# Walking the slices of d_ff two by two in a fused attention and MLP kernel

## The chip, the cores and the metric

The kernel runs on one core of one Trainium2 chip. The metric is the device time of one execution in microseconds. Five engines work side by side, each through its own instructions in order: PE (TensorE, matmuls; PEld is its loading of the stationary operand), DVE (VectorE), ACT (ScalarE), POOL (GpSimd) and SP (SyncE, which here issues nearly all DMAs).

## The reference

```python
# q, k, v: (4, 8, 768, 64); banded attention with 8 global and 96 local keys, slopes by head
scores = scale * q @ k.T + bias                    # bias = -slope * distance
a = softmax(where(keep, scores, -1e9))             # keep: the band and the global keys
attn_out = a @ v
x = attn_out.transpose(0, 2, 1, 3).reshape(3072, 512)
h = x @ w_in                                       # w_in: (512, 2048)
g = h * clip(h + 3, 0, 6) / 6
out = g @ w_out                                    # w_out: (2048, 512)
```

## The kernel before, in words

The 3072 tokens are eight blocks of 384. For a block, four pairs of heads are attended, each giving 128 rows of the transposed x; then the MLP runs over 16 slices of d_ff, 128 columns each. A matmul operand is split in a high and a low part, both in fp32r, and three of the four products are summed. Per slice that makes:

- the first layer (`first`, L167): four k-tiles by three products, 12 matmuls of 128x128 by 128x384 into one PSUM tile `hp`. There are two `hp` banks.
- the gate: ACT takes relu(h+3) into `g` (L178), DVE makes min(g, 6)\*h (L179), POOL copies the high part `gh` (L185) and DVE takes the rest `gl` = g - gh (L192). There is one `g` tile (pool `gp1`); `gh` and `gl` have three buffers each (pool `gp`).
- the second layer (`second`, L199): three tiles of 128 tokens by three products, 9 matmuls with 512 output columns, into the three `acc` tiles (for the second block, the tiles `sp`, `tp` and `xp`).

`halves` walks the slices with a lag of one: first layer of slice f, a yield, then the second layer of slice f-1 (`finish`), a yield. After the last slice of a block `finish` also stores the block: three ACT copies to tiles `o` (pool `op`, three buffers), three DMAs. The lag goes over the edge of a block: the last slice of a block gets its second layer inside the first slice of the next.

At each yield the caller hangs in a unit of the attention for the block after: `attention` spreads four pairs over 30 units, six a pair. Units 0, 1 and 2 of a pair are the score matmuls of the token tiles t = 0, 1, 2 (L842, four matmuls each) with their weighing (DVE L853, ACT L857); unit 3 splits the next pair's q and k (`kx` on POOL L813), sums up and normalizes two tiles (POOL L877), unit 4 normalizes the third and spreads the first, unit 5 spreads the others and fetches. `spread` turns the softmax rows by DVE in blocks of 32 (L902) and writes them to DRAM by a DMA (L904, `there<-blocks`); `fetch` reads them back, transposed, by four DMAs (L911, `weights<-there`). At the ends of the second and the fourth pair (units 17 and 29) `values` multiplies those weights by v for two pairs (L929, here called values) and writes x. During the last eight slices of the second block `rest_of_third` does the same for the third block in coarser units.

A scheduler orders DVE and ACT; PE, SP and POOL keep the order in which the program is written (`in_order`). The weights are decoded from int64 words during the first 155 us, on DVE above all; in that time the slices of the first two blocks go in an order written by hand (`ORDER`), and that part stays as it is.

Of the kernel before, what the change touches and what calls it, by code (L numbers as in the profile page):

```python
# [25 lines left out]
NF = DF // P  # L26
# [33 lines left out]
class Kernel:  # L60
# [45 lines left out]
    def common(self, xs, banks):  # L106
        self.xp = self.pool("xp", xs)
        self.w1h, self.w1l, self.w2h, self.w2l = [], [], [], []
        self.gp = self.pool("gp", 3)
        self.gp1 = self.pool("gp1", 1)  # L110
        self.ps_h = self.pool("ps_h", banks, PSUM)

# [174 lines left out]
    def load(self, n, values):  # L287

        if n < len(self.blocks) * NPAIR:
            end = KW + (TB if n < EARLY else QW)  # L290
            for columns in (slice(KW + QW, LOAD),) if values else (slice(0, KW), slice(KW, end)) if n == 0 else (slice(0, end),):
                self.nc.sync.dma_start(out=self.place(n)[:, columns], in_=self.pairs[n, :, columns])
# [155 lines left out]
    def halves(self, steps, pool=False):  # L448


        for block, f, x, acc in steps:
# [11 lines left out]
                yield  # L463
            self.last = (block, f, acc, gh, gl)

    def end(self, steps):

        x, acc = steps[0][2:]
        late = []
        for k, (_, f, _, _) in enumerate(steps):  # L470
            g = self.gate(self.first(f, x), f == NF - 1)
            gh = self.high(g, True)
            late.append((f, acc, gh, self.rest(g, gh)))
            if k == 0:
                self.finish()
            elif k == 1:
                self.second(*late[0], (0, 1))
        self.second(*late[0], (2,))
        self.second(*late[1], (0, 1))
        self.second(*late[2], (0, 1))  # L480
        self.second(*late[1], (2,))
        self.second(*late[2], (2,))
# [11 lines left out]
    def banded(self, flag):  # L494
# [12 lines left out]
        with ExitStack() as early, ExitStack() as words:  # L507
            x0 = self.x_tiles(self.pool("x0", 1, ctx=early, side="right"))
            xs = [x0, self.x_tiles(), self.x_tiles()]
# [7 lines left out]
            acc = []  # L517
# [62 lines left out]
            acc1 = [pool.tile([P, BANK], F32, name=name) for pool, name in ((self.ps_s, "sp"), (self.ps_t, "tp"), (self.ps_x, "xp"))]  # L580
            self.given[1] = max(self.given)
            next_f, todo = [FIRST, 0], []
# [6 lines left out]
        self.attending(self.ctx, 2, 3, 2, side="right")  # L589
        self.bp = self.pool("bp", 3, side="right")  # L590
        self.there = self.pool("there", 2, bass.MemoryType.DRAM)
        self.op = self.pool("op", 3, side="right")
        self.stage = "one"
        units, pairs = self.rest_of_third(xs[2], NF - next_f[1])
        for k, _ in enumerate(self.halves([(1, f, xs[1], acc1) for f in range(next_f[1], NF)], True)):
            for unit in units[k]:
                unit()
        self.finish()
        pairs[-2].values("s")
        self.stage = "layers"  # L600
        x, ahead = xs[2], pairs[-1]
        for i in range(2, len(self.blocks)):
            units, x_next = [], None
            if i + 1 < len(self.blocks):
                x_next = self.x_tiles()
                units, ahead = self.attention(i + 1, x_next, ahead)
            else:
                units = [[]] * 4 + [[lambda: self.doubt(flag)]]
            acc = self.acc_tiles()
            steps = [(i, f, x, acc) for f in range(NF)]  # L610
            for k, _ in enumerate(self.halves(steps if x_next else steps[:-3], True)):
                for unit in units[k] if k < len(units) else ():
                    unit()
            if not x_next:
                self.end(steps[-3:])
            x = x_next
# [392 lines left out]
```

## Time and profile before

| | |
|---|---|
| median of 3 runs | 663.02 us (662.13 to 663.42) |
| span of the profiled execution | 660.9 us, from its first to its last instruction |
| PE | 649.6 us busy, 98% of the span |
| PEld | 581.9 us, 88% |
| DVE | 427.6 us, 65% |
| ACT | 288.1 us, 44% |
| POOL | 202.2 us, 31% |

The profile is of one execution. Its time by the clock that gave the three runs isn't listed, so durations are set against the span of 660.9 us; the median is 2.1 us above it. Busy times overlap: matmuls are pipelined, a row's duration is longer than the distance from its start to the next one's, so the pace of PE is read from starts. The word "pitch" stands for that distance below.

### The profile page before, as it was taken

The numbers are of one execution on the slowest core, as the hardware profiler recorded it, in microseconds if no ns is written. First come the engines' busy times: TensorE is split into PE (matmuls) and PEld (weight loads), VectorE is DVE, ScalarE is ACT, GpSimd is POOL, SyncE is SP. The second block draws the span as 40 slices with busy tenths as digits, with TensorE's granted clock in tenths as the row PEclk, the third lists the DMA queues.
The fourth block names the chain that finished last, engine by engine and source line by source line (L and its number), as shares of the span: only waits on it lengthen the run. The fifth ranks groups of instructions, "written<-read, shape, count | busy, mean of one in ns | idle before, by whom it ended". The sixth has DMA issues, their size and how long they took to land.

```text
span 660.9 us, 11414 instructions
## 1 busy us (share of the span) xinstructions
PE 649.6 (98%) x3933; PEld 581.9 (88%) x3933; DVE 427.6 (65%) x1147; ACT 288.1 (44%) x752; POOL 202.2 (31%) x377
## 2 busy tenths in 40 slices
PE   9989999999999999999999999999999999999997
PEld 7768899998989999999989999899998999989995
DVE  6888999998856876367654777367663777422222
ACT  6896877776434343344314333143422443121111
POOL 5663000002533433034331553134340444312110
PEclk9999999999999999999999999999999999999999
DMA  8676445432582566536553557615654265510001
GB/s 284 178 233 215 132 157 159 132 124 89 158 224 95 156 175 172 143 100 162 153 153 96 135 137 185 180 51 143 165 138 128 95 160 131 133 49 1 1 1 53
DMA packets 67316, 88.86 MB, mean 134 GB/s; under 512 B 10288, under 2 KB 52016, under 8 KB 67248
## 3 DMA queue, kind: packets, MB, share of 16 engines
q1 hardware_dynamic: 66960, 87.77, 46.5%
q8 instruction: 33, 0.54, 0.3%
q14 instruction: 35, 0.29, 0.1%
q10 hardware_dynamic: 288, 0.26, 0.1%
HBM read 65.08 MB, written 22.94 MB: 133 GB/s over the span
## 4 chain that ended last, share of the span: by engine, by line
PE 86%; DVE 9%; ACT 2%; issue 2%; POOL 0%; POOLq 0%; DVEq 0%; ACTq 0%
PE hp L167 37%; PE acc L199 33%; PE xp L929 3%; PE sp L842 2%; PE tp L929 2%; PE tp L842 2%; PE sp L199 1%; ACT n L857 1%; DVE wz L422 1%; PE tp L199 1%; DVE wz L418 1%; PE xp L199 1%; DVE wz L410 1%; DVE g L179 1%; DVE gl L192 1%
## 5 line engine op out<-in xcount | busy, mean ns | idle before, releaser
L178 ACT ACTIVATE g<-hp,small 128x384 f32<-128x384 f32 x127 | 73.7, 580 | 253.3 <-PE hp L167 227.0
L167 PE MATMUL hp<-xh,w1h 128*128 128x384 f32 x512 | 174.1, 340 | 0.4 <-ACT w1h L426 0.4
L167 PE MATMUL hp<-xh,w1l 128*128 128x384 f32 x512 | 173.0, 338 | 0.5 <-DVE w1l L415 0.5
L167 PE MATMUL hp<-xl,w1h 128*128 128x384 f32 x512 | 171.9, 336 | 0.0
L185 POOL TENSOR_SCALAR gh<-g 128x384 fp32r<-128x384 f32 x104 | 55.6, 535 | 311.2 <-DVE g L179 279.7
L199 PE MATMUL acc<-w2h,gl 128*128 128x512 f32 x336 | 133.2, 396 | 0.2 <-DVE gl L192 0.2
L199 PE MATMUL acc<-w2l,gh 128*128 128x512 f32 x336 | 132.4, 394 | 0.0
L199 PE MATMUL acc<-w2h,gh 128*128 128x512 f32 x336 | 131.9, 393 | 0.0
L179 DVE SCALAR_TENSOR_TENSOR g<-g,hp 128x384 f32<-128x384 f32 x128 | 69.8, 545 | 69.7 <-ACT g L178 69.1
L877 POOL TENSOR_SCALAR n<-n,sums 128x232 f32<-128x232 f32 (+1 forms) x186 | 99.4, 549 | 32.2 <-DVE sums L868 17.6
L192 DVE TENSOR_TENSOR gl<-g,gh 128x384 fp32r<-128x384 f32 x128 | 78.4, 613 | 47.5 <-POOL gh L185 47.5
L857 ACT ACTIVATE n<-n,least 128x232 f32<-128x232 f32 (+1 forms) x192 | 89.0, 465 | 41.6 <-DVE least L853 40.3
L167 PEld LDWEIGHTS hp<-xh,w1h 128*128 128x128 f32 x512 | 96.3, 188 | 6.4 <-issue 1.7
L167 PEld LDWEIGHTS hp<-xl,w1h 128*128 128x128 f32 x512 | 96.2, 188 | 3.8
L167 PEld LDWEIGHTS hp<-xh,w1l 128*128 128x128 f32 x512 | 96.0, 188 | 1.0 <-DVE w1l L415 0.8
L199 PEld LDWEIGHTS acc<-w2h,gl 128*128 128x128 f32 x336 | 63.0, 187 | 15.1 <-DVE gl L192 1.6
L199 PEld LDWEIGHTS acc<-w2h,gh 128*128 128x128 f32 x336 | 63.3, 188 | 10.5 <-POOL gh L185 0.3
L199 PEld LDWEIGHTS acc<-w2l,gh 128*128 128x128 f32 x336 | 63.2, 188 | 10.3
L902 DVE STREAM_TRANSPOSE blocks<-n 128x256 f32<-128x256 f32 x127 | 48.8, 422 | 27.0 <-POOL n L877 26.8
L813 POOL TENSOR_SCALAR kx<-load 64x504 fp32r<-64x504 f32 (+1 forms) x46 | 35.3, 767 | 100.3 <-PE hp L167 96.2
L853 DVE CUSTOM_DVE_ANT_0 n<-sp,d 128x232 f32<-128x232 f32 (+1 forms) x70 | 23.7, 376 | 36.7 <-PE sp L842 36.5
L857 ACT ACTIVATION_READ_ACCUMULATOR n<-n,least 128x1 f32 x192 | 36.1, 188 | 0.0
(118 smaller groups left out, 746.4 us busy)
## 6 DMA issues: line engine op xcount, KB each, us to landing
wst<-w SPq DMA_DIRECT2D x32, 512.0 KB, 3.5
there<-blocks SPq DMA_DIRECT2D x58, 256.0 KB, 2.6
load<-pairs SPq DMA_DIRECT2D x23, 636.0 KB, 5.1
load<-pairs SPq DMA_DIRECT2D x32, 384.0 KB, 4.3
weights<-there SPq DMA_DIRECT2D x48, 192.0 KB, 3.8
weights<-there SPq DMA_DIRECT2D x44, 160.0 KB, 3.2
out<-o SPq DMA_DIRECT2D x23, 256.0 KB, 2.2
load<-pairs SPq DMA_DIRECT2D x8, 444.0 KB, 4.4
```

Of the source, the lines that this page charges most:

```text
L167: self.nc.tensor.matmul(hp, lhsT=self.w1(w, f)[:, kt, :], rhs=a[:, kt, :], start=(n == 0), stop=(n == 3 * NKT - 1))
L178: nc.scalar.activation(out=g, in_=hp, func=AF.Relu, bias=self.three, scale=1.0)
L179: nc.vector.scalar_tensor_tensor(out=g, in0=g, scalar=6.0, in1=hp, op0=ALU.min, op1=ALU.mult)
L185: self.nc.gpsimd.tensor_scalar(out=gh, in0=g, scalar1=1.0, scalar2=0.0, op0=ALU.mult, op1=ALU.add)
L192: self.nc.vector.tensor_tensor(out=gl, in0=g, in1=gh.bitcast(F32), op=ALU.subtract)
L199: self.nc.tensor.matmul(acc[tt], lhsT=a[:, tk], rhs=self.w2(w, f), start=(f == 0 and j == 0), stop=(f == NF - 1 and j == 2))
L813: nc.gpsimd.tensor_scalar(out=part["kx"][own, c], in0=k[own, c], scalar1=1.0, scalar2=0.0, op0=ALU.mult, op1=ALU.add)
L842: nc.tensor.matmul(sp[j][:, lo:W], lhsT=q[:, t], rhs=part["kx"][:, c], start=(m == 0), stop=(m == 1))
L857: nc.scalar.activation(out=e[:, j, lo:W], in_=e[:, j, lo:W], func=AF.Exp, bias=self.least[:, i:i + 1], scale=-1.0, accum_out=self.sums[:, ...
L877: nc.gpsimd.tensor_scalar(out=e[:, j, lo:W], in0=e[:, j, lo:W], scalar1=over, scalar2=0.0, op0=ALU.mult, op1=ALU.add)
L902: nc.vector.transpose(out=blocks[:, :, s].rearrange("p b j q -> p j b q"), in_=e[:, :, c:c + P].rearrange("p j (b q) -> p j b q", b=4))
L929: nc.tensor.matmul(xps[j * D:(j + 1) * D, t * P:(t + 1) * P], lhsT=vt[0:K, t, j * D:(j + 1) * D], rhs=self.part(t, j, c, K), start=(c == 0 ...
```

## The change

A new walker `twos` takes the slices in pairs: both first layers with their gates, two yields, then the second layers of the pair before, two yields. It takes the place of `halves` from slice 8 of the second block to the end, but for the last three slices of the last block, which `end` still walks one by one. `gh` and `gl` get a fourth buffer each, and `o` goes from three buffers to two to make room. No instruction is added or taken away: each engine issues the same number of each operation up to the end of this path.

```diff
-        self.gp = self.pool("gp", 3)
+        self.gp = self.pool("gp", 4)
...
+    def twos(self, steps, pool=False):
+        for i in range(0, len(steps), 2):
+            after = []
+            for block, f, x, acc in steps[i:i + 2]:
+                self.decoded_to(2 * f)
+                g = self.gate(self.first(f, x))
+                gh = self.high(g, pool)
+                after.append((block, f, acc, gh, self.rest(g, gh)))
+                self.work(2.1, 0.94)
+                if i == 0 and len(self.pending) == 1:
+                    self.last = self.pending[0]
+                    self.finish()
+                    self.pending = []
+            yield
+            yield
+            for self.last in self.pending:
+                self.finish()
+            self.pending = after
+            yield
+            yield
...
     def end(self, steps):
...
             if k == 0:
-                self.finish()
+                for self.last in self.pending:
+                    self.finish()
...
-        self.op = self.pool("op", 3, side="right")
+        self.op = self.pool("op", 2, side="right")
...
-        for k, _ in enumerate(self.halves([(1, f, xs[1], acc1) for f in range(next_f[1], NF)], True)):
+        self.pending = [self.last]
+        for k, _ in enumerate(self.twos([(1, f, xs[1], acc1) for f in range(next_f[1], NF)], True)):
...
-        self.finish()
+        for self.last in self.pending:
+            self.finish()
+        self.pending = []
...
-            for k, _ in enumerate(self.halves(steps if x_next else steps[:-3], True)):
+            for k, _ in enumerate(self.twos(steps if x_next else steps[:-3], True)):
```

On PE, in a late block, before: the end of a slice's first layer (tile `hp_5570`) and the second layer of the slice before it.

```order
L167 MATMUL hp_5570<-xh_4119,w1h1_1023 128x384
L167 MATMUL hp_5570<-xl_4120,w1h1_1023 128x384
L167 MATMUL hp_5570<-xh_4119,w1l1_1024 128x384
L199 MATMUL acc_4951<-w2h1_1025,gh_5531 128x512
L199 MATMUL acc_4951<-w2l1_1026,gh_5531 128x512
L199 MATMUL acc_4951<-w2h1_1025,gl_5543 128x512
```

On PE after, in the same block: the end of a first layer is followed by the next slice's.

```order
L167 MATMUL hp_5506<-xh_4110,w1h1_1023 128x384
L167 MATMUL hp_5506<-xl_4111,w1h1_1023 128x384
L167 MATMUL hp_5506<-xh_4110,w1l1_1024 128x384
L167 MATMUL hp_5526<-xh_4110,w1h1_1023 128x384
L167 MATMUL hp_5526<-xl_4111,w1h1_1023 128x384
L167 MATMUL hp_5526<-xh_4110,w1l1_1024 128x384
```

The runs of one kind are now 24 and 18 matmuls long instead of 12 and 9. From slice 8 of the second block on there were 104 runs of first layers and 104 of second layers; now there are 55 and 54. The score matmuls, which stood between them four at a time, stand eight and four at a time: `yield` follows on `yield`, so units 0 and 1 of a pair come together.

On POOL, around the normalizing of the last pair of heads of a block, before (`kx` of the next pair, `n` the softmax rows, `gh` the gates):

```order
L185 TENSOR_SCALAR gh<-g 128x384 x2
L813 TENSOR_SCALAR kx<-load_73 64x504 x2
L877 TENSOR_SCALAR n<-n,sums 128x128 x2
L877 TENSOR_SCALAR n<-n,sums 128x232 x2
L185 TENSOR_SCALAR gh<-g 128x384
L877 TENSOR_SCALAR n<-n,sums 128x232 x2
```

On POOL after, at the same place:

```order
L185 TENSOR_SCALAR gh<-g 128x384 x2
L839 TENSOR_SCALAR kx<-load_73 64x504 x2
L903 TENSOR_SCALAR n<-n,sums 128x128 x2
L903 TENSOR_SCALAR n<-n,sums 128x232 x4
L185 TENSOR_SCALAR gh<-g 128x384 x6
```

The six normalizings now follow on each other; before, a gate's copy stood ahead of the last two.

On DVE, at the same pair, before: from the split of the next pair's q (the two rows on L816) to the turning of the softmax rows (`blocks`).

```order
L816 SCALAR_TENSOR_TENSOR q_5555<-load_73,q_5554 128x384
L816 SCALAR_TENSOR_TENSOR q_5560<-load_73,q_5559 128x384
L192 TENSOR_TENSOR gl<-g,gh 128x384
L867 TENSOR_SCALAR sums<-sums 128x6
L819 TENSOR_TENSOR kx<-load_73,kx 64x504
L868 RECIPROCAL sums<-sums 128x6
L819 TENSOR_TENSOR kx<-load_73,kx 64x504
L902 STREAM_TRANSPOSE blocks<-n 128x2x4x32
L179 SCALAR_TENSOR_TENSOR g<-g,hp 128x384
L902 STREAM_TRANSPOSE blocks<-n 128x2x4x32 x2
L192 TENSOR_TENSOR gl<-g,gh 128x384
L902 STREAM_TRANSPOSE blocks<-n 128x2x4x32 x2
```

On DVE after:

```order
L842 SCALAR_TENSOR_TENSOR q_5556<-load_73,q_5555 128x384
L842 SCALAR_TENSOR_TENSOR q_5561<-load_73,q_5560 128x384
L179 SCALAR_TENSOR_TENSOR g<-g,hp 128x384
L893 TENSOR_SCALAR sums<-sums 128x6
L894 RECIPROCAL sums<-sums 128x6
L192 TENSOR_TENSOR gl<-g,gh 128x384
L845 TENSOR_TENSOR kx<-load_73,kx 64x504 x2
L928 STREAM_TRANSPOSE blocks<-n 128x2x4x32 x5
```

The gate of the second slice of the pair now stands ahead of the sums, the reciprocal no longer behind a split of `kx`, and no gate between the turnings.

## The prediction, made before the changed kernel ran

> **What bounds the kernel now.** I read the busy times first, then the same by stretches of the part that changes, then the pitch of PE's matmuls in the timeline, and last the chain that feeds the values. The page says that PE is busy for 98% of the span:
>
> ```profile
> PE 649.6 (98%) x3933; PEld 581.9 (88%) x3933; DVE 427.6 (65%) x1147; ACT 288.1 (44%) x752; POOL 202.2 (31%) x377
> ```
>
> The view by stretches shows that in the changed part it is all of it. Columns: stretch, its length, then busy time and count for PE, PEld, DVE, ACT, POOL, the granted clock, DMA share, GB/s.
>
> ```profile
> 155.00:330.00 175.00, 175.00 (x1069) 158.50 (x1068) 116.20 (x332) 70.79 (x208) 63.69 (x117) 1.00 0.55 153
> 330.00:500.00 170.00, 170.00 (x1019) 154.53 (x1018) 104.06 (x276) 57.62 (x162) 62.47 (x107) 1.00 0.51 141
> 500.00:650.00 150.00, 150.00 (x870) 135.92 (x869) 67.86 (x167) 39.59 (x99) 37.89 (x72) 1.00 0.26 71
> ```
>
> From 155 to 650 us PE has no idle time, at full clock; beside PE's own weight loading no engine passes 70% in any stretch. So there is no wait to remove. The change can gain only if a matmul starts sooner after the one before it, and it can lose only by making PE wait. Busy durations don't tell the first, since they overlap; the starts do. Starts in late blocks and around 155 us (start, duration, engine, line):
>
> ```profile
> 152.94 0.39 PE L199 MATMUL acc<-w2h,gh 128*128 128x512 f32 x1
> ...
> 154.09 0.39 PE L199 MATMUL acc<-w2h,gl 128*128 128x512 f32 x1
> ...
> 155.00 0.33 PE L167 MATMUL hp<-xh,w1h 128*128 128x384 f32 x1
> ...
> 195.82 0.39 PE L199 MATMUL sp<-w2l,gh 128*128 128x512 f32 x1
> ...
> 197.41 0.39 PE L199 MATMUL xp<-w2h,gl 128*128 128x512 f32 x1
> ...
> 603.31 0.33 PE L167 MATMUL hp<-xh,w1h 128*128 128x384 f32 x1
> ...
> 615.87 0.33 PE L167 MATMUL hp<-xh,w1h 128*128 128x384 f32 x1
> ...
> 616.93 0.33 PE L167 MATMUL hp<-xh,w1h 128*128 128x384 f32 x1
> ...
> 617.97 0.39 PE L199 MATMUL acc<-w2h,gh 128*128 128x512 f32 x1
> ...
> 645.17 0.33 PE L167 MATMUL hp<-xh,w1h 128*128 128x384 f32 x1
> ```
>
> Three things stand there. From 603.31 to 645.17 lie ten slices without attention: 41.86/10 = 4.186 us for 12 first-layer and 9 second-layer matmuls. Inside a run of first layers (615.87 to 617.97) the first six take 1.06 us, 177 ns each, and the last six 1.04 us, 173 ns each: the run begins slowly and settles. Second layers do the same, later: from 152.94 five take 1.15 us, 230 ns each, and the last four (154.09 to 155.00) 0.91 us, 227 ns each; in the run that begins after attention work, seven pitches from 195.82 to 197.41 are 1.59 us, 227 ns each, settled from its second matmul on. So a change of kind costs something at the start of the run that follows, and a run twice as long should pay it once for two.
>
> **The change part by part.**
>
> Runs of PE. At settled pitch a slice would take 12 x 173 ns + 9 x 227 ns = 2.08 + 2.04 = 4.12 us, against 4.186: 0.066 us is the slow starts of its two runs. I take 0.060, since rounding to 10 ns leaves that much open (0.050 to 0.070). The built order loses 49 runs of first layers (104 to 55) and 50 of second layers (104 to 54). 50 x 0.060 = 3.0 us, all of it on PE's path, as nothing else covers a busy PE. From below: if runs of 24 and 18 stay slow for longer, the gain falls to 0; from above: 50 x 0.070 = 3.5 us. I take 3.0, because each run seen so far settles before its end.
>
> Gates and scores. The four steps of a gate and the reading of a score tile are on the page (mean ns of one in the last column but one):
>
> ```profile
> L178 ACT ACTIVATE g<-hp,small 128x384 f32<-128x384 f32 x127 | 73.7, 580 | 253.3 <-PE hp L167 227.0
> L185 POOL TENSOR_SCALAR gh<-g 128x384 fp32r<-128x384 f32 x104 | 55.6, 535 | 311.2 <-DVE g L179 279.7
> L179 DVE SCALAR_TENSOR_TENSOR g<-g,hp 128x384 f32<-128x384 f32 x128 | 69.8, 545 | 69.7 <-ACT g L178 69.1
> L192 DVE TENSOR_TENSOR gl<-g,gh 128x384 fp32r<-128x384 f32 x128 | 78.4, 613 | 47.5 <-POOL gh L185 47.5
> ...
> L853 DVE CUSTOM_DVE_ANT_0 n<-sp,d 128x232 f32<-128x232 f32 (+1 forms) x70 | 23.7, 376 | 36.7 <-PE sp L842 36.5
> ```
>
> One gate is 0.58 + 0.55 + 0.54 + 0.61 = 2.3 us, and there is one `g`, so two slices' gates follow each other. First layers of the pair end 2.1 us apart; the second slice's `hp` bank is free some 1.4 us after its end even if its relu waits 0.2 us for `g`, and its `gh` and `gl` are there after 2.5 us. The bank is wanted again after a run of 18 (4.12 us) and one of 12 (2.1), and the second layers only after 8 us. Before, a slice had 4.2 us for the same 2.3. So gates get more slack, and queueing of several us on POOL or DVE behind them stays hidden. The fourth buffers of `gh` and `gl` are what two slices in flight need; they cost nothing.
>
> Score matmuls by eight and four: the same count, on two banks in turn. A bank is used again a run of 24 or 18 later (over 4 us), while DVE's reading of a tile costs twice 0.38 us (last row). Nothing; if DVE were late there, PE would wait for `sp` or `tp`.
>
> Store with two `o` tiles. The third copy on ACT must wait for the first tile's DMA:
>
> ```profile
> out<-o SPq DMA_DIRECT2D x23, 256.0 KB, 2.2
> ```
>
> 2.2 us, less what the second copy takes, so ACT stands for about 2 us, six times. Behind it on ACT are weighings and the relu of the next pair, with the slack just counted; the `acc` tile that it holds is wanted after 24 first layers, 4.2 us. Hidden; if ACT were late by 2 us more, PE would wait for `acc`.
>
> Attention's chain to the values. This is the part with the least room. Each number of a unit stays, but its time moves. For the fourth pair of a block the last scores (unit 20) come at the end of a run of 24 instead of after the first of two single runs, and the values (unit 29) are then four long runs away. Before, the way is this (PE, POOL, DVE, SP, and the landing times of the last two fetch DMAs from the tile's view, then their median from the page):
>
> ```profile
> 404.48 0.61 PE L842 MATMUL sp<-kx,q 128*128 128x232 f32 x4
> 404.92 0.39 PE L199 MATMUL acc<-w2h,gh 128*128 128x512 f32 x1
> ...
> 423.85 1.54 PE L929 MATMUL xp<-weights,load 128*64 128x128 f32 x24
> 425.22 1.05 PE L929 MATMUL tp<-weights,load 128*64 128x128 f32 x16
> ...
> 406.23 1.32 DVE L816 SCALAR_TENSOR_TENSOR q<-load,q 128x384 fp32r<-128x384 f32 x2
> ...
> 409.78 2.04 POOL L877 TENSOR_SCALAR n<-n,sums 128x232 f32<-128x232 f32 x4 [1.05 <-DVE sums L868]
> ...
> 412.77 1.29 POOL L877 TENSOR_SCALAR n<-n,sums 128x232 f32<-128x232 f32 x2
> ...
> 414.10 0.77 DVE L902 STREAM_TRANSPOSE blocks<-n 128x256 f32<-128x256 f32 x2 [0.71 <-POOL n L877]
> ...
> 417.58 1.73 SPq L911 DMA_DIRECT2D weights<-there  x4
> ...
> DMA to landing us min/median/max: 3.8/4.3/4.9
> ...
> weights<-there SPq DMA_DIRECT2D x48, 192.0 KB, 3.8
> ```
>
> The fourth DMA goes out in the last quarter of the 1.73 us after 417.58, near 418.9, and lands 4.9 us later, at 423.8; the matmuls that read it start at 425.22. So 1.4 us are left, 20.7 us after the scores. After the change that distance is 0.44 (scores, 404.48 to 404.92) + 4.12 + 4.18 + 4.12 + 4.18 (the four runs) + 1.37 (the third pair's values) = 18.4 us, 2.3 us less. The chain, now 423.8 - 404.5 = 19.3 us, gets shorter too: the six normalizings take from 409.78 to 414.06, 4.3 us, with a gate's copy in their midst; in a row they take 2.04 x 6/4 = 3.1, 1.2 us less. But the gate of the pair's second slice now goes behind DVE's split of q (1.32 us), and POOL's `kx` and normalizings behind that gate; of this POOL's idle time before the normalizings (1.05 us) takes up all but 0.3, and I put in 0.5. So 19.3 - 0.7 = 18.6 against 18.4: 0.2 us of waiting in this block, which has one of the slowest landings (4.9 against a median of 3.8). In the others I expect none. Five blocks have such a place; I put in 0.3 us, between 0 and 3. For the first two pairs (units 8 and 17) three more times 0.44 us of scores lie on the way, 19.7 us: no wait.
>
> The sum against the profiled execution: 660.9 - 3.0 + 0.3 = 658.2 us of span. The median of the runs lies 2.1 us above that span, so 660.3 us.
>
> A rule of the Trainium skill speaks against the first term. "TensorE: Matmul & The Clock Gate", section "Back-to-back issue gap", gives a matmul's distance to the next by its moving size alone, N/2.4 + 2.5 ns: 162.5 ns for 384 columns and 215.8 for 512. By it the order of the same matmuls changes nothing, and the sum would be the 663.0 us of now (with the waits, 663.3). The settled pitches above, 173 and 227 ns, lie 11 ns over it and the starting ones more, so the trace disagrees on the size and on there being one value only.
>
> **The rivals.**
>
> *No gain from longer runs.* The slow start is not a cost of the change of kind but, say, of where each slice's tiles lie, and comes back at each slice: PE's order is then worth nothing, and 663.0 + 0.3 = 663.3 us (662.4 to 664.3). For it: all matmuls of a slice share tiles. Against it: the second layers at 195.82, which follow on attention work, start settled with the same kind of tiles. The Trainium skill's rule above ends here as well.
>
> *The values wait for their weights* (slower). If the chain doesn't get shorter but longer, because the two gates of a pair, 1.2 us of DVE each, now stand in one heap in front of the sums, then 19.3 + 1.2 = 20.5 against 18.4: 2.1 us in five places and 0.8 us (20.5 - 19.7) in five others, 14.5 us, less 3.0: 674.5 us; with 19.3 unchanged, 0.9 x 5 - 3.0 = 1.5 us slower, 664.5 us. It decides from a mean chain of about 19.0 us on, where waits of 0.6 us in five places make 3.0. For it: the 1.4 us that are left now. Against it: the order of DVE, in which the reciprocal moves ahead of `kx`, and a median landing that is 1 us quicker. I price it at 666.5 (664.3 to 674.5).
>
> *The tiles lie worse.* The fourth buffers move all weights by 2 x 1536 = 3072 bytes. That a place can matter shows in the first block's x, which lies in a pool of its own:
>
> ```profile
> 132.56 0.34 PE L167 MATMUL hp<-xh,w1h 128*128 128x384 f32 x1
> ...
> 134.68 0.40 PE L199 MATMUL sp<-w2h,gh 128*128 128x512 f32 x1
> ```
>
> There a run of 12 takes 2.12 us, 177 ns each, and doesn't settle. If all long runs did so, the 100 slices that go in pairs would lose 12 x (177 - 173) = 0.05 us each, 4.8 us, but for the slow starts that they then don't have (0.02 each): some 3 us, which eats the gain: 663.3 us. [...]
>
> **How the numbers follow.** The forecast has 0.70, with a range of its own from 659.3 (3.5 gained, no wait, and 0.2 for the spread of the runs) to 661.7. No gain has 0.13, worse places 0.05, waiting values 0.12. The predicted time is 660.3 us. The range runs from 659.2 to 663.8 us: it takes in the forecast and most of the two cases near 663.3 and leaves out the waits. 0.2% is 1.3 us, about what a measurement of this kernel can tell from no change: under 661.7 is faster, over 664.3 slower. Faster 0.70, same 0.18, slower 0.12.
>
> **What the profile after would show.** Right: from 155 to 645 us PE is as full as now; a run of 24 first layers lasts 4.18 us from start to start and its second twelve 2.08; a run of 18 second layers 4.12 and its second nine 2.04; two slices without attention take 8.31 instead of 8.37 us. The wait for `weights<-there` ahead of the values stays under 0.3 us a place. Wrong: second halves of runs at 177 or 231 ns (no gain), all of a run at 177 (places), gaps of PE ahead of the second values of a block (waits), or any gap ahead of `hp`, `acc` or the scores, which would mean that I misjudged the gates, the store or the banks.

## The result and the profile after

The changed kernel takes 667.69 us (median of 4 runs, 666.06 to 667.94), the kernel before 662.95 us beside it (4 runs, 662.13 to 663.42). The ratio is 1.0067, with a 95% interval of 1.0053 to 1.0081: slower by some 4.5 us, where 660.3 us and a gain were forecast. The profiled execution took 667.92 us, with a span of 666.0 us against 660.9.

Busy times of the page hardly move: PE has 649.2 us where it had 649.6, in a span that is 5.1 us longer.

```profile
PE 649.2 (97%) x3933; PEld 582.1 (87%) x3933; DVE 423.7 (64%) x1147; ACT 286.5 (43%) x752; POOL 189.3 (28%) x377
```

So PE idles more. Where, the view by stretches tells; its columns are the stretch, its length, busy time and count of PE, PEld, DVE, ACT and POOL, granted clock, DMA share, GB/s. First the kernel before, then the changed one:

```profile
154.30:184.00 29.70, 29.70 (x179) 26.92 (x178) 23.45 (x78) 16.39 (x53) 11.20 (x22) 1.00 0.48 141
184.00:214.00 30.00, 30.00 (x183) 26.65 (x182) 17.70 (x41) 10.59 (x27) 10.17 (x18) 1.00 0.58 171
```

```profile
154.30:184.00 29.70, 28.98 (x174) 25.99 (x173) 23.59 (x76) 15.83 (x49) 10.94 (x22) 1.00 0.47 137
184.00:214.00 30.00, 25.17 (x148) 21.93 (x147) 13.10 (x34) 8.65 (x24) 7.09 (x14) 0.94 0.63 175
214.00:605.00 391.00, 390.98 (x2383) 356.26 (x2383) 234.87 (x642) 135.63 (x387) 125.10 (x239) 1.00 0.49 133
```

From 214 to 605 us, nearly all of the late blocks, PE is as full as ever. All the idle time is in the 60 us in which the second block ends and the third begins: 59.70 - 28.98 - 25.17 = 5.55 us, none before. In the second of these stretches the granted clock is 0.94 as well. PE's waits from 150 us on (what waits, for which engine's which tile, us in all, times, longest):

```profile
PE hp L167 <- ACT xh L153: 2.6, 1, 2.6
PE acc L955 <- DMA weights<-there: 1.7, 1, 1.7
PE acc L868 <- DVE kx L845: 0.6, 2, 0.4
PE hp L167 <- DVE w1l L415: 0.5, 1, 0.5
PE sp L868 <- DVE least L879: 0.4, 1, 0.4
```

The wait for `w1l` stands in the kernel before as well (0.5 us); the other four are new. The largest, for `xh`, is ACT's doing (ACT's timeline, changed kernel):

```profile
196.86 0.60 ACT L56 ACTIVATE o<-sp 128x512 f32<-128x512 f32 x1 [2.50 <-PE sp L199]
197.54 0.60 ACT L56 ACTIVATE o<-tp 128x512 f32<-128x512 f32 x1
204.56 0.60 ACT L56 ACTIVATE o<-xp 128x512 f32<-128x512 f32 x1 [6.42 <-DMA out<-o]
205.05 0.47 ACT L153 CAST xh<-acc 128x384 fp32r<-128x384 f32 x1
```

The third copy of the second block's store needs one of the two `o` tiles back. ACT waits 6.42 us for the first store DMA, and behind it stands the copy of the last quarter of the third block's x. With three tiles the same copies went through at once:

```profile
196.47 0.60 ACT L56 ACTIVATE o<-sp 128x512 f32<-128x512 f32 x1 [0.40 <-PE sp L199]
197.16 0.60 ACT L56 ACTIVATE o<-tp 128x512 f32<-128x512 f32 x1
197.83 0.60 ACT L56 ACTIVATE o<-xp 128x512 f32<-128x512 f32 x1
199.09 0.48 ACT L153 CAST xh<-acc 128x384 fp32r<-128x384 f32 x1 [0.66 <-PE acc L929]
```

Why the DMA is so late stands on SP (issue times, changed kernel) and in the view of the tile `o` between 195 and 206 us (a landing is the time from a DMA's issue until its data has arrived):

```profile
186.02 0.84 SPq L292 DMA_DIRECT2D load<-pairs  x2
186.90 2.45 SPq L930 DMA_DIRECT2D there<-blocks  x3
194.62 1.76 SPq L937 DMA_DIRECT2D weights<-there  x4
196.48 0.84 SPq L292 DMA_DIRECT2D load<-pairs  x2
197.49 8.03 SPq L57 DMA_DIRECT2D out<-o  x3
```

```profile
DMA to landing us min/median/max: 2.1/6.9/7.0
```

Two loads are issued 0.6 to 1.0 us ahead of the first store DMA, and that lands after 7.0 us. The third store DMA, issued after the loads are through (205.18), takes 2.1. That the loads make the first store late is read from these landings; no run moves the loads away from the store. The same view of the kernel before, whose second load was issued 1.5 us after the first and whose stores follow 1.5 us later, has this, and nobody waited:

```profile
DMA to landing us min/median/max: 4.4/5.3/5.4
```

PE around that wait (start, duration, engine, line; the wait in brackets), and the granted clock us by us (stretch, PE busy and count, clock, DMA share, GB/s):

```profile
197.79 0.39 PE L199 MATMUL xp<-w2h,gl 128*128 128x512 f32 x1
199.89 1.32 PE L955 MATMUL acc<-weights,load 128*64 128x128 f32 x20 [1.71 <-DMA weights<-there]
...
202.63 0.34 PE L167 MATMUL hp<-xh,w1l 128*128 128x384 f32 x1
205.57 0.45 PE L167 MATMUL hp<-xh,w1h 128*128 128x384 f32 x1 [2.60 <-ACT xh L153]
206.17 0.48 PE L167 MATMUL hp<-xl,w1h 128*128 128x384 f32 x1
...
209.92 0.34 PE L167 MATMUL hp<-xl,w1h 128*128 128x384 f32 x1
```

```profile
206.00:207.00 1.00, 0.85 (x4) 0.72 1.28 318
207.00:208.00 1.00, 1.00 (x4) 0.50 0.72 237
208.00:209.00 1.00, 1.00 (x4) 0.50 0.26 101
209.00:210.00 1.00, 1.00 (x5) 0.57 0.00 0
```

Nine matmuls of the third block's first slice run, the tenth is the first that needs the late quarter of x, and it starts 2.94 us after the ninth. Then the clock is at half for 0.56 + 1 + 1 + 0.86 = 3.42 us (a mean of 0.72 in a microsecond is 0.56 of it at 0.5), and most matmuls stand 0.32 us apart instead of 0.17: from 206.17 to 209.92 there are twelve distances in 3.75 us, where twelve at 0.174 make 2.09, so 1.7 us are lost.

### The profile page after: what moved, and what is told of

Same layout as the page of the kernel before. It is cut to its first block, busy times and chain, and to the rows that moved or that the text cites. A ratio compares the mean times of both kernels' runs of the same rounds, so it can differ in the third digit from the quotient of the medians.

```text
span 666.0 us, 11404 instructions
## 1 busy us (share of the span) xinstructions
PE 649.2 (97%) x3933; PEld 582.1 (87%) x3933; DVE 423.7 (64%) x1147; ACT 286.5 (43%) x752; POOL 189.3 (28%) x377
## 4 chain that ended last, share of the span: by engine, by line
PE 82%; DVE 10%; issue 3%; ACT 2%; POOL 1%; DMA 1%; POOLq 0%; ACTq 0%; DVEq 0%
PE hp L167 35%; PE acc L199 33%; PE xp L955 3%; PE sp L868 2%; PE tp L955 2%; PE tp L868 2%; DVE wz L422 1%; DVE wz L418 1%; ACT n L883 1%; PE sp L199 1%; DMA out<-o 1%; DVE gl L192 1%; DVE n L879 1%; PE tp L199 1%; PE xp L199 1%
## 5 line engine op out<-in xcount | busy, mean ns | idle before, releaser
L185 POOL TENSOR_SCALAR gh<-g 128x384 fp32r<-128x384 f32 x104 | 53.3, 512 | 292.8 <-DVE g L179 258.2
L903 POOL TENSOR_SCALAR n<-n,sums 128x232 f32<-128x232 f32 (+1 forms) x186 | 94.3, 524 | 53.7 <-DVE sums L894 44.2
L192 DVE TENSOR_TENSOR gl<-g,gh 128x384 fp32r<-128x384 f32 x128 | 75.9, 593 | 49.2 <-POOL gh L185 49.0
L839 POOL TENSOR_SCALAR kx<-load 64x504 fp32r<-64x504 f32 (+1 forms) x46 | 29.3, 636 | 115.9 <-PE hp L167 96.1
```

Source lines behind the costliest of these rows:

```text
L185: self.nc.gpsimd.tensor_scalar(out=gh, in0=g, scalar1=1.0, scalar2=0.0, op0=ALU.mult, op1=ALU.add)
L192: self.nc.vector.tensor_tensor(out=gl, in0=g, in1=gh.bitcast(F32), op=ALU.subtract)
L839: nc.gpsimd.tensor_scalar(out=part["kx"][own, c], in0=k[own, c], scalar1=1.0, scalar2=0.0, op0=ALU.mult, op1=ALU.add)
L903: nc.gpsimd.tensor_scalar(out=e[:, j, lo:W], in0=e[:, j, lo:W], scalar1=over, scalar2=0.0, op0=ALU.mult, op1=ALU.add)
```

## The experiments

The kernel before ran beside each group: 662.48 us (27 runs) beside the first four, 663.06 us (23 runs) beside the last three. My theory after the result was that the two `o` tiles make the largest wait; the rivals were that the order of the second block's end does it, and that larger pools put tiles in worse places.

**The sizes alone.** The kernel before with nothing but the pool sizes of the change.

```diff
-        self.gp = self.pool("gp", 3)
+        self.gp = self.pool("gp", 4)
-        self.op = self.pool("op", 3, side="right")
+        self.op = self.pool("op", 2, side="right")
```

> The kernel before with only the pool sizes of the change: four gh and gl, two o; order as before. Theory A (the store): at the end of the second block the third copy of the store waits for the landing of the first out DMA (at 201.5 us in the trace of before), and the last x copy stands behind it on ACT; PE then wants x at about 200.6 and gets it at about 202.7: a gap of some 2 us, 665 us, or 667 if the clock falls after it. Theory B (the order alone makes the waits): no gap, 663.0. If the tiles lay worse, runs of first layers would take 2.12 us instead of 2.10.

Measured: 665.82 us, ratio 1.0049 (1.0032 to 1.0065). The sizes alone, without a single matmul in another order, cost 3.3 us. ACT's timeline and PE's wait of this kernel:

```profile
201.46 0.60 ACT L56 ACTIVATE o<-xp 128x512 f32<-128x512 f32 x1 [3.74 <-DMA out<-o]
```

```profile
202.48 0.45 PE L167 MATMUL hp<-xh,w1h 128*128 128x384 f32 x1 [1.70 <-ACT xh L153]
```

The same copy waits for the same DMA, 3.74 us, PE for 1.70, and the clock is at half from 203.70 us on, for 3.42 us. The runs of this kernel fall in two groups: four of 663.9 to 665.0 us with a mean granted clock of 0.999 or 1.000, four of 666.6 to 668.0 with 0.997. The profiled run is of the second group. The mean clock doesn't tell where in a run the half clock fell, so it fits, but isn't shown, that it follows on this wait in about every second execution.

**Twos from the third block on.** The changed kernel, but slices 8 to 15 of the second block go one by one as before.

```diff
-        self.pending = [self.last]
-        for k, _ in enumerate(self.twos([(1, f, xs[1], acc1) for f in range(next_f[1], NF)], True)):
+        for k, _ in enumerate(self.halves([(1, f, xs[1], acc1) for f in range(next_f[1], NF)], True)):
...
-        for self.last in self.pending:
-            self.finish()
+        self.finish()
```

> The pairs of slices only from the third block on; the last slices of the second block one by one as before; four gh and gl, two o. Theory A: the gap of the store is there as with the sizes alone, the long runs give back 2.5 us: 662.5 to 664.5. Theory B: 660.5, since the order of the second block is as before. If long runs gave nothing: as the sizes alone.

Measured: 665.76 us, ratio 1.0045 (1.0027 to 1.0063), more than I expected. The wait for `xh` is 2.9 us in this kernel's profile and the half clock follows, so the gain of the long runs is used up once more. The waits for weights and for `kx` ahead of 200 us are gone, which ties those to the second block's new order; but that order is not the main cause.

**A third store tile.** The changed kernel, in which the first two blocks' stores take their third tile from the pool of `blocks` (same shape, three buffers, idle at that time).

```diff
...
+            if tt == NT - 1:
+                o = self.bp.tile([P, 4, 2, 2, 32], F32, name="blocks").rearrange("p b s j q -> p (b s j q)")
+            else:
+                o = self.op.tile([P, DM], F32, name="o")
...
```

> The changed kernel, but in the stores of the first two blocks the third tile is borrowed from the pool of the softmax blocks (2048 bytes as well), so that no copy waits for an out DMA. Theory A: the gap ahead of x (3.2 us), the half clock after it (1.7) and the late scores (0.5) go: 662.3. The wait of the second block's last values for their weights (1.9 us) stays. Theory B: the gap stays with another releaser, 667.

Measured: 664.02 us, ratio 1.0026 (1.0017 to 1.0035), span 661.4. In the profile, the wait for `xh` and the half clock are gone. Each set against the kernel before beside it, the medians fall from 4.7 us above it to 1.5, some 3 us; the 662.3 us expected were 1.7 us lower still. What stays is mainly the values' wait, 1.2 us here:

```profile
PE acc L965 <- DMA weights<-there: 1.2, 1, 1.2
PE acc L878 <- DVE kx L855: 0.6, 2, 0.4
```

**Third tile, and twos from the third block on.** Both edits together.

> Both: the second block one by one as before, pairs of slices from the third block on, and the borrowed third tile in the first two stores. Theory A and B: no waits left, long runs alone: 660.4 (2.6 us under before). If long runs gave nothing: 663.

Measured: 661.13 us, ratio 0.9968 (0.9953 to 0.9984): faster than before, by 2.1 us by the ratio and 1.4 by the medians, and the best of all versions. Its order is the change's in the late blocks, where the forecast saw the gain.

**Halves with the sizes and the third tile.** The base for the one just shown: same sizes, same tile, no twos.

> The order of the kernel before (slice by slice) with the changed kernel's sizes (four tiles each of gh and gl, two of o) and the third store tile borrowed in the first two blocks. If the two o tiles are all that the sizes cost, this is the kernel before again: 662.5 us, where the sizes alone gave 665.8. It is also the base against which the late twos are measured: with the same sizes and tile, twos from the third block on gave 661.1, so their own gain would be 1.4 us of the 2.4 that 40 pairs of slices at 0.060 us make, less about 1.1 us of waits. If the sizes cost something else, it stays above 664 us.

Measured: 662.91 us, ratio 0.9998 (0.9989 to 1.0006), the kernel before again. So the two `o` tiles are all that the sizes cost, and tiles in other places cost nothing that this measurement can tell (0.1%). The ratios 0.9968 and 0.9998 put the twos of the late blocks at 0.3%, 2.0 us; by the medians it is 1.2 us, and the two intervals together leave some 1 to 3. (The expectation spoke of 40 pairs; of the 50 runs that fall away, the second block's four pairs have 4, so 46 is right.)

**Keeping PE awake.** The changed kernel with 11 products of constants (22 matmul rows in the trace) in the wait for `xh`.

```diff
+                if n == 9 and self.extra:
+                    self.spin(self.extra)
+                    self.extra = 0
...
```

> The changed kernel with 11 products of constants (the f32 128x128 products that keep TensorE running at the start, about 0.23 us each) between the ninth and the tenth matmul of the third block's first slice, where TensorE had stood idle for 2.9 us and the granted clock was 0.5 for 3.4 us afterwards. Nothing waits less: the tenth matmul still needs xh from ScalarE at the same time. If the half clock follows from the idle time, the clock is 1.0 all through, the 12 or so matmuls of 320 ns cost 174 again, and the time is about 1.7 us less than the changed kernel's: 666.0 us against before's 662.5 (ratio 1.005). If the half clock comes from something else (a power limit at that place), it stays, and the time is 667.7 us.

Measured: 666.46 us, ratio 1.0063 (1.0041 to 1.0086; 6 runs, too few to tell it from the changed kernel by time). The trace tells it. PE at that place, and the clock:

```profile
203.26 2.62 PE L366 MATMUL acc<-small 128*128 128x128 f32 x22
205.63 0.42 PE L171 MATMUL hp<-xh,w1h 128*128 128x384 f32 x1
...
659.38 0.39 PE L203 MATMUL acc<-w2h,gl 128*128 128x512 f32 x1
```

```profile
202.00:212.00 10.00, 9.62 (x68) 1.00 0.36 116
```

The clock stays at 1.00, with the tenth matmul as late as in the changed kernel (205.63 and 205.57). From there to the last second-layer matmul it takes 659.38 - 205.63 = 453.75 us; in the changed kernel, whose last one is this,

```profile
660.86 0.40 PE L199 MATMUL acc<-w2h,gl 128*128 128x512 f32 x1
```

660.86 - 205.57 = 455.29, 1.5 us more. At the place itself the difference is larger: to the first matmul of the next slice it takes 210.32 - 205.63 = 4.69 us, in the changed kernel 212.24 - 205.57 = 6.67. Of these 2.0 us, 0.34 is the first distance after the wait (0.26 against 0.60) and the rest the clock; 0.4 us is lost again later. Of the six runs, four have a mean clock of 0.998 to 1.000, where the changed kernel's four all have 0.996. So the half clock followed from the idle time, and cost 1.6 to 1.7 us. The median shows less of it, in part because the products themselves took time: ACT had the last copy of x ready at 204.50 + 0.47 = 204.97, and they held PE until 205.63.

**One load behind the weights.** The version with the third tile; besides, the 636 KB load that stood ahead of the spreads of the third block's last weights is issued behind their fetch.

```diff
-            ... after.split(k))
+            ... after.split(k, after is not pairs[2]))
+        units[11].append(lambda: self.load_next(pairs[2].n, False))
```

> The changed kernel with a third store tile in the first two blocks, as before, and the 636 KB load of the second pair of block 4 issued behind the fetch of the third block's last weights instead of ahead of their spreads. If those spreads landed late (193.0 to 194.5 us) because the queue held two loads of 1 MB together ahead of them, they land about 2 us sooner, the weights by about 197.5, and the 1.3 us wait of the last values goes: 662.7 us against 664.0 with the third tile alone. If the spreads are late because the rows that they carry are late on VectorE, or because the landing does not depend on what is queued ahead, nothing moves: 664.0 us.

Measured: 661.97 us, ratio 0.9984 (0.9976 to 0.9993): faster than before. The two versions ran in different groups; each set against the kernel before beside it, this one is 2.6 us (medians) or 2.8 us (ratios) below the third tile alone, where 1.3 were expected. The profiled spans, 660.1 and 661.4 us, differ by 1.3, but the other one is of the fastest of its 12 runs; the rest isn't explained. SP with the third tile alone, and here:

```profile
186.04 0.84 SPq L302 DMA_DIRECT2D load<-pairs  x2
186.92 2.30 SPq L940 DMA_DIRECT2D there<-blocks  x3
194.11 1.76 SPq L947 DMA_DIRECT2D weights<-there  x4
```

```profile
186.63 0.38 SPq L302 DMA_DIRECT2D load<-pairs  x1
187.07 2.57 SPq L941 DMA_DIRECT2D there<-blocks  x3
192.97 1.74 SPq L948 DMA_DIRECT2D weights<-there  x4
```

The spreads go out no sooner, but they land after 3.8 to 4.3 us instead of 5.4 to 5.6; the fetch, which waits for that, goes out at 192.97 instead of 194.11, and PE doesn't wait for these weights any more. What was queued ahead of the spreads made them late.

## Why the prediction was wrong

*Runs of PE (-3.0 us): right, and slightly too large.* A run of 24 first layers in the changed kernel:

```profile
230.18 0.33 PE L167 MATMUL hp<-xh,w1h 128*128 128x384 f32 x1
...
232.29 0.34 PE L167 MATMUL hp<-xh,w1h 128*128 128x384 f32 x1
...
234.37 0.60 PE L868 MATMUL sp<-kx,q 128*128 128x232 f32 x4
```

4.19 us in all (4.18 forecast): 2.11 us for the first twelve and 2.08, the number forecast, for the second. Over four blocks, from the first matmul of the fourth block to that of the eighth, before and in the version with the third tile:

```profile
275.32 0.34 PE L167 MATMUL hp<-xh,w1h 128*128 128x384 f32 x1
...
586.47 0.33 PE L167 MATMUL hp<-xh,w1h 128*128 128x384 f32 x1
```

```profile
275.68 0.33 PE L168 MATMUL hp<-xh,w1h 128*128 128x384 f32 x1
...
585.11 0.33 PE L168 MATMUL hp<-xh,w1h 128*128 128x384 f32 x1
```

311.15 and 309.43 us: 1.72 less for 32 pairs of slices, 0.054 a pair where 0.060 was put in, so 2.7 us for 50. (In the changed kernel itself the same stretch has 309.67 us, with a short wait of one block's values in it.) The first rival (no gain) falls with it, and so do places of tiles. On the rule that the prediction set beside this rival: the Trainium skill, "TensorE: Matmul & The Clock Gate", section "Back-to-back issue gap", gives its formula for an isolated matmul and says that in a stream the loading of the stationary operand counts too, so it doesn't rule out that order matters.

*Gates (0): right.* From 150 us on, no wait of PE is for a gate.

*Scores (0): wrong by about 1 us.* Eight score matmuls in a row wait once for DVE's reading (`least`, 0.4 us), as the text named it. In the second block's end they wait for the split of `kx` (0.6 us in two places), which the step didn't consider: there the units are coarser, and DVE has weighings and gates to do ahead of the split. These waits were read in the trace only, not taken away by themselves.

*Store with two `o` tiles (hidden): the step that failed.* It had two errors. The landing was priced at 2.2 us, the profile page's median over 23 DMAs. That held at the other six stores ahead of the last one (2.0 to 2.3 us, one DMA 3.5), and ACT waited at two of them only, for 1.5 and 1.6 us, without any wait of PE. At the end of the second block two loads are ahead: 7.0 us. The tile's view of the kernel before showed 4.4 to 5.4 us there. And the list of what stands behind the copy on ACT had the weighings and the relu but not the copy of x, which the tenth matmul of the third block reads; room was seen for 24 first layers, and there was room for nine matmuls. The text's own sign for this, a gap ahead of `hp`, is what the profile shows. This cost 2.6 us of idle time, and some 3 us in medians together with what follows on it.

*The clock: not in the sum at all.* It cost 1.6 to 1.7 us. A forecast of any wait of PE of 2 us should have carried it.

*Attention's chain to the values (+0.3): right where it looked, wrong in scope.* PE idles 0.02 us between 214 and 605, and in one place the values' second half starts 0.2 us late; in the three versions with twos and the third tile one such place waits 0.4 to 0.5 us, near the 0.3 put in. But the text counted five late places with a distance of 18.4 us and left out the second block's end. There two loads go out just ahead of the spreads, which land after 5.7 to 6.1 us where the changed kernel's median is 2.6, and the values wait 1.7 us. The rival "the values wait for their weights" had this mechanism, but its price was for the late blocks.

Against the forecast's span of 658.2 us: 5.55 us of idle time, of which 0.3 was forecast, 1.7 for the clock, and 0.3 us for the smaller gain make 665.4, of 666.0 measured. Of the other 0.6 us, 0.4 is the first distance after the wait (205.57 to 206.17 is 0.60 us where 0.17 is usual); the rest stays open.

## What to carry to other kernels

When a change takes a buffer away to make room, price it at its tightest place: the landing of that very DMA with what is queued ahead of it, not a median, and every instruction behind the one that waits. Here an edit of one digit cost more than the reordering of 100 runs gave, and giving the buffer back from a pool that was idle just then turned a loss of 0.7% into a gain of 0.3%, with the order kept to the blocks that had slack. A stall of PE costs more than its length, since the clock may follow.

## What was new about the hardware

*The clock falls after short gaps.* The profiles' idle times of PE ahead of half clock were 2.6 us (changed kernel), 2.9 (twos from the third block), 1.70 (sizes alone) and, in the first block of the kernel that was kept awake, this one:

```profile
43.93 1.86 PE L961 MATMUL xp<-pt,load 128*64 128x128 f32 x24 [1.91 <-issue]
```

Idle times of 1.71 us (changed kernel, ahead of the values) and 1.2 us were followed by none, and one of 1.91 us at this same place in the version with third tile and late twos neither. Between 1.7 and 1.9 us it went both ways. The fall came 0.9 to 1.2 us after PE had started again (206.44 after 205.57, 203.70 after 202.48, 45.00 after 43.93). The Trainium skill, "TensorE: Matmul & The Clock Gate", section "What's actually happening", describes a free-running window of about 3.4 us, over which activity decides. The stretches of half clock here, 3.41 to 3.42 us in the four profiles that have one in these places, agree, and so does that equal gaps end differently. Its section "Why this matters for your kernels" allows gaps up to about 3 us; here 1.70 us was once enough, so the measurement differs.

*A small DMA lands behind the large ones ahead of it.* A 256 KB store landed after 2.1 us alone and after 7.0 us behind two loads on the same queue. The Trainium skill, "DMA: Bandwidth & Descriptors", section "Queues, rings and completion order", says that each DMA engine takes a queue's descriptors in order and that a completion is reported only after that engine's earlier writes; the spreads that landed after 3.8 to 4.3 us instead of 5.4 to 5.6, once one of the two loads ahead was moved behind their fetch, agree.
